# A new order for all engines in the 256-token pair stage, and sums written back into PSUM

## The chip, the cores and the metric

The kernel runs on one core of a Trainium2 chip. Its engines run their own instruction streams, each in order, and wait for one another by semaphores: TensorE (PE in the profile; PEld is its weight load), VectorE (DVE), ScalarE (ACT), GpSimd (POOL) and SyncE (SP, which here only issues DMAs). The metric is the device time of one execution in microseconds (us).

## The reference

A Fourier mixing layer over 8 x 3008 tokens of 256 channels is followed by a gated feed-forward network:

```python
X = np.fft.rfft(x, axis=1)
...                                   # complex linear map, soft threshold, inverse transform
gate = 1.0 / (1.0 + np.exp(-(x @ w_gate)))
val = x @ w_val
return (gate * val @ w_out).astype(np.float32)
```

Here x has 24064 tokens, w_gate and w_val are 256 x 1536 and w_out is 1536 x 256. The Fourier part and the first 4608 tokens of the network fill the first 1025 us or so. The other 19456 tokens go through the pair stage, and the change lies there.

## The kernel before

The pair stage takes 38 pairs of 2 x 256 tokens (NPR). For each pair it runs NH = 6 slots, one for each block of 256 hidden units, so there are 228 slots (NU). In a slot both matrix products of the network are done by a seven-product scheme for 2 x 2 blocks (Strassen's, in Winograd's form) instead of eight products. All values are kept as a high part and a remainder (fp32r), so each product of two blocks takes three matmuls: high by high, high by remainder, remainder by high.

In this text M1 to M7 are the first layer's products of a slot (`first`, each 2 x 3 = 6 matmuls of 128 x 256), and s1 to s7 the second layer's (`second`, 3 matmuls each). That makes 7 x 6 + 7 x 3 = 63 matmuls a slot.

- The first layer accumulates in four PSUM banks of 512 columns: M1 then M2 into bank a (pa), M5 into bank c (pc), M6 and M3 into bank b (pb), M7 and M4 into bank d (pd). ScalarE copies between banks, which the scheme needs as starting values: a to b behind M1 (here called seedb), b to d behind M6 (seedd), both in `seed`.
- Out of the banks come four hidden blocks. Each bank half pair is gate and value: the gate goes through a sigmoid on ScalarE (g11, g21 and so on), the product of gate and value is VectorE's (h11, h21, h12, h22). For the second column M5 must be added first: `take_m5` copies bank c into an SBUF tile m5, and `column2` adds it to bank d and to bank b (here X22 and X12), into the SBUF tile xg. One activation (`gate2`) and one product (`h2`) of 512 columns follow.
- GpSimd makes the four sums of hidden blocks that the second layer needs (`hsum`, S1, S3, S2, S4).
- Then the operands are split: ScalarE casts the high part (`hi`: hiX, hiG, hiS; tiles hpX, hpG, hpS), VectorE subtracts for the remainder (`lo`: loX, loG, loS).
- The second layer accumulates over the six slots of a pair in four more banks (acc). At a pair's end they are evicted (`evict1` to `evict4`): ScalarE copies, VectorE sums, three stores on SP and one adding store on GpSimd's queue.
- During three slots of each pair the next pair's input tile ypair is prepared (`prep_steps`): GpSimd sums, a cast on ScalarE, a remainder on VectorE.

The order of the stage is written out by hand in `slot(k)`, under a manual schedule: slot k issues the first layer of block k, sums, casts and remainders of block k-1, and the second layer of block k-2. On TensorE the order is M1, M5, s1, s2, M6, M2, s4, M7, M3, s7, s6, s5, M4, s3. M4 adds to bank d, which X22 must have read.

Of the kernel before, what the change touches and what calls it, by code (L numbers as in the profile page):

```python
# [26 lines left out]
HW = 256  # L27
# [83 lines left out]
def tile_fft_mix_ffn(ctx: ExitStack, tc, x, w_r, w_i, b_r, b_i, w_one, w_out, mf, mi, mis, fa, fb, mf0, fa0, out):  # L111
# [529 lines left out]
    def prep_steps(p, sub_):  # L641
        g = nc.gpsimd

        def sums(i):
            y = held["y", p]
# [12 lines left out]
        def split(v, names):  # L658
            v = v().rearrange("p a n -> p (a n)")
            t = p4.tile([P, 2, len(names) * HW], F32R, tag=f"xop{len(names)}", bufs=NXB if len(names) == 2 else 2,  # L660
                        name=names[0])
            nc.scalar.copy(t[:, 0], v)
            sub_(t[:, 1], v, t[:, 0])
            xs[p].update(halves_of(t, names))

        return [lambda: sums(1), lambda: split(lambda: held["y", p][:, 1], ("a12", "a22")),
                lambda: sums(3), lambda: split(lambda: held["y", p][:, 0], ("a11", "s3")),
                lambda: (sums(2), sums(4)), lambda: split(lambda: held["s", p], ("s1", "s2", "s4"))]

    hx, hop, accs = {}, {}, {}  # L670
    NU = NPR * NH
# [16 lines left out]
    def second(k, *names):  # L688
        if not 0 <= k < NU:
            return  # L690
        p, fp = divmod(k, NH)
        if p not in accs:
            accs[p] = [psg.tile([P, 512], F32, tag="acc", bufs=2, name="acc") for _ in range(2)]
        w = weights2(fp)
        for name in names:
            b, h = ACC[name]
            if b == len(accs[p]):
                accs[p] += [bank("acc2", "l2", L2_BANKS) for _ in range(2)]
            o = accs[p][b][:, h * HW:(h + 1) * HW]
            xn, wn = PRODUCTS[name]  # L700
            (hh, hl), (wh, wl) = hop[k].pop(xn), w[wn]
            for l, r in ((wh, hh), (wh, hl), (wl, hh)):
                start = fp == 0 and name in (1, 4, 6, 3) and l is wh and r is hh
                nc.tensor.matmul(o, l, r, start=start, stop=l is wl, skip_group_check=True)  # L704
# [8 lines left out]
    def gate(o):  # L713
        nc.scalar.activation(o, o, AF.Sigmoid)  # L714

    def gate11(k):
        g = hx[k, "G"] = p5.tile([P, 2, HW], F32, name="gh", bufs=2)
        nc.scalar.activation(g[:, 0], bank_a[:, :HW], AF.Sigmoid)

    def h11(k):  # L720
        g = hx[k, "G"]
        nc.vector.tensor_mul(g[:, 0], g[:, 0], bank_a[:, HW:])  # L722

    def gate21(k):
# [13 lines left out]

    def gate2(k):
        gate(hx[k, "X"][:, 0])  # L740

    def h2(k):
        x = hx[k, "X"]
        nc.vector.tensor_mul(x[:, 0], x[:, 0], x[:, 1])  # L744

    def hsum(k, i, e):

        x, g = hx[k, "X"], hx[k, "G"]
        if i == 1:
            hx[k, "S"] = p5.tile([P, 3, HW], F32, name="hs", bufs=2)  # L750
            e.tensor_add(hx[k, "S"][:, 0], g[:, 1], x[:, 0, 1])  # L751
# [4 lines left out]
        else:  # L756
            e.tensor_sub(hx[k, "S"][:, 2], x[:, 0, 0], hx[k, "S"][:, 1])  # L757

    def parts_of(k, what):
        v = hx[k, "X"][:, 0] if what == "X" else hx[k, what]  # L760
        return v.rearrange("p a n -> p (a n)")
# [17 lines left out]
    def ev_tile():  # L779
        return p5.tile([P, 7 * HW + PAD], F32, name="ev", bufs=1)[:, :7 * HW].rearrange("p (a n) -> p a n", n=HW)  # L780

    def evict1(p):
        ev = held["ev", p] = ev_tile()
        nc.scalar.copy(ev[:, 0:2].rearrange("p a n -> p (a n)"), accs[p][0])
        nc.sync.dma_start(out_of(p)[:, 0, :HW], ev[:, 0])

    def evict2(p):
        ev, acc = held["ev", p], accs[p]
        nc.vector.tensor_add(ev[:, 5], acc[2][:, :HW], ev[:, 0])
        nc.vector.tensor_add(ev[:, 6], acc[1][:, HW:], ev[:, 5])  # L790
        for ct, lot, i in (0, 1, 6), (1, 0, 5), (1, 1, 6):
            nc.sync.dma_start(out_of(p)[:, ct, lot * HW:(lot + 1) * HW], ev[:, i])
        nc.scalar.copy(ev[:, 2], acc[1][:, :HW])

    def evict3(p):
        ev, acc = held["ev", p], accs[p]
        nc.scalar.copy(ev[:, 4], acc[2][:, HW:])
        nc.vector.tensor_add(ev[:, 3], acc[3][:, :HW], ev[:, 4])

    def evict4(p):  # L800
        nc.gpsimd.dma_start(out_of(p), held["ev", p][:, 1:5].rearrange("p (t a) n -> p t (a n)", t=CT), accum_op=ALU.add)

    def evict_last(p):
        ev, acc = held["ev", p], accs[p]
        add = nc.vector.tensor_add
        add(ev[:, 5], acc[2][:, :HW], ev[:, 0])
        add(ev[:, 6], acc[1][:, HW:], ev[:, 5])
        nc.gpsimd.tensor_add(ev[:, 1], ev[:, 0], ev[:, 1])
        add(ev[:, 2], acc[1][:, :HW], ev[:, 6])
        nc.sync.dma_start(out_of(p)[:, 0], ev[:, 1:3].rearrange("p a n -> p (a n)"))  # L810
        add(ev[:, 5], acc[2][:, HW:], ev[:, 5])
        add(ev[:, 4], acc[2][:, HW:], ev[:, 6])
        add(ev[:, 3], acc[3][:, :HW], ev[:, 5])
        nc.sync.dma_start(out_of(p)[:, 1], ev[:, 3:5].rearrange("p a n -> p (a n)"))

    def slot(k):

        v, g = nc.vector, nc.gpsimd
        live, before = k < NU, 0 < k <= NU
        p, e = divmod(k, NH)  # L820
        q = k - 2
        ends = q >= 0 and q % NH == NH - 1
        begins = q > 0 and q % NH == 0
        qp = q // NH
        last = k >= NU
        steps = None
        if live and p + 1 < NPR:
            if e == 0:
                load_y(p + 1)
                held["prep", p + 1] = prep_steps(p + 1, sub)  # L830
            steps = held["prep", p + 1]
        if live and k:
            first(k, 1)
            seed(bank_b, bank_a)
            first(k, 5)
        if begins:
            evict2(qp - 1)
        if before:
            for i in 1, 3, 2, 4:
# [430 lines left out]
```

## Time and profile before

| | before |
|---|---|
| time, median of 3 runs | 2844.3 us (2842.35 to 2847.09) |
| the profiled execution | 2846.19 us, span 2844.4 us |
| PE busy | 2744.1 us, 96% of the span |
| PEld, DVE, ACT, POOL busy | 88%, 72%, 62%, 41% |
| mean granted TensorE clock | 0.995 |

The span is the time from the first to the last instruction in the profile. The shares are means over the whole program, which has stages of different limits. From about 1070 us on all is pair stage. Matmuls are pipelined, and the profile models their ends: the duration of one is longer than the distance to the next.

### The profile page before, as it was taken

The page shows a single profiled execution, that of the slowest core. Times are in us where ns is not written, and L with a number is a line of the kernel's source. Part 1 is how long each engine was busy: PE and PEld are TensorE (multiplying, and loading weights), DVE is VectorE, ACT ScalarE, POOL GpSimd, SP SyncE. Part 2 cuts the span into 40 slices and gives each one's busy share as a digit, 9 for nine tenths or more (in the row PEclk, how much of TensorE's full clock was granted, in tenths as well). Part 3 has the DMA queues.
Part 4 walks back from the last instruction along what each step waited for, and adds up shares of the span by engine and source line. Part 5 has one row for each costly group of instructions (what it writes and reads, how often), then busy time and mean ns, then how long its engine had stood idle before and what let it go on. Part 6 is the DMA issues. An engine that isn't in the chain of part 4 may idle for free.

```text
span 2844.4 us, 60508 instructions
## 1 busy us (share of the span) xinstructions
PE 2744.1 (96%) x24208; PEld 2508.0 (88%) x24208; DVE 2059.9 (72%) x3240; ACT 1757.1 (62%) x3302; POOL 1153.9 (41%) x1399
## 2 busy tenths in 40 slices
PE   8999999999999999999999999999999999999998
PEld 6678888888998789999999999999999999999998
DVE  5777887777776257777777777777777777777777
ACT  4665655555655356666666666666666666666665
POOL 0231021336000025555555555555555555555554
PEclk9999999999999999999999999999999999999999
DMA  9877656776555731111111111111101111101111
GB/s 288 258 239 197 176 170 172 222 210 209 167 158 164 211 87 27 42 25 44 25 44 25 44 25 44 25 44 25 44 23 46 23 46 23 46 23 45 24 38 25
DMA packets 200873, 268.29 MB, mean 94 GB/s; under 512 B 19664, under 2 KB 152272, under 8 KB 200592
## 3 DMA queue, kind: packets, MB, share of 16 engines
q1 hardware_dynamic: 179504, 220.04, 26.1%
q0 software_dynamic: 20832, 44.31, 7.3%
q8 instruction: 191, 3.13, 0.5%
q14 instruction: 90, 0.74, 0.1%
q10 hardware_dynamic: 256, 0.07, 0.0%
HBM read 137.33 MB, written 127.01 MB: 93 GB/s over the span
## 4 chain that ended last, share of the span: by engine, by line
PE 50%; DVE 25%; POOL 12%; ACT 6%; issue 4%; DMA 3%; SPq 0%; DVEq 0%; ACTq 0%; POOLq 0%
PE pd L684 6%; PE acc L704 6%; PE pa L684 5%; PE pb L684 5%; PE pm L307 5%; DVE xg L736 4%; POOL gh L755 3%; PE pc L684 3%; DVE xg L744 2%; PE pb L274 2%; DVE gh L722 2%; PE pia L390 2%; DVE hpG L772 2%; POOL hs L751 2%; DVE hpS L772 2%
## 5 line engine op out<-in xcount | busy, mean ns | idle before, releaser
L751 POOL TENSOR_TENSOR hs<-gh,xg 128x256 f32<-128x256 f32 x227 | 167.2, 737 | 790.7 <-DVE gh L729 790.7
L772 DVE TENSOR_TENSOR hpG<-gh,hpG 128x512 fp32r<-128x512 f32 x228 | 241.5, 1059 | 258.1 <-ACT hpG L768 258.1
L684 PE MATMUL pd<-a,th 128*128 128x256 f32 x1824 | 366.5, 294 | 50.3 <-DVE xg L736 41.6
L684 PEld LDWEIGHTS pd<-a,th 128*128 128x128 f32 x1824 | 275.6, 188 | 101.4 <-DVE xg L736 88.7
L684 PE MATMUL pa<-a,w1h 128*128 128x256 f32 x1824 | 336.7, 278 | 0.0
L772 DVE TENSOR_TENSOR hpX<-xg,hpX 128x512 fp32r<-128x512 f32 x228 | 197.9, 868 | 157.1 <-ACT hpX L768 157.1
L684 PEld LDWEIGHTS pa<-a,w1h 128*128 128x128 f32 x1824 | 275.9, 188 | 0.0
L755 POOL TENSOR_TENSOR gh<-gh 128x256 f32<-128x256 f32 x227 | 247.0, 1088 | 17.8
L684 PE MATMUL pd<-a,tl 128*128 128x256 f32 x912 | 253.8, 278 | 0.0
L684 PE MATMUL pa<-a,w1l 128*128 128x256 f32 x912 | 252.7, 277 | 0.0
L772 DVE TENSOR_TENSOR hpS<-hs,hpS 128x768 fp32r<-128x768 f32 x228 | 244.6, 1073 | 0.0
L704 PE MATMUL acc<-hpS,w 128*128 128x256 f32 x1368 | 234.3, 280 | 0.0
L757 POOL TENSOR_TENSOR hs<-xg,hs 128x256 f32<-128x256 f32 x227 | 214.2, 944 | 17.8
L768 ACT CAST hpS<-hs 128x768 fp32r<-128x768 f32 x228 | 192.8, 845 | 46.4 <-POOL hs L757 44.8
L714 ACT ACTIVATE xg<-xg 128x512 f32<-128x512 f32 x228 | 144.0, 632 | 116.4 <-DVE xg L736 112.7
L707 ACT COPY pd<-pb 128x512 f32<-128x512 f32 x228 | 130.7, 573 | 135.0 <-ACT hpX L768 91.8
L684 PE MATMUL pb<-s,th 128*128 128x256 f32 x912 | 175.9, 286 | 20.1 <-ACT pb L707 20.1
L704 PEld LDWEIGHTS acc<-hpS,w 128*128 128x128 f32 x1368 | 192.5, 188 | 0.0
L307 PE MATMUL pm<-w_sb,xsh 128*128 128x256 f32 x1008 | 184.6, 285 | 2.2 <-ACT xsh L290 1.6
L707 ACT COPY pb<-pa 128x512 f32<-128x512 f32 x228 | 131.3, 576 | 87.5 <-PE pa L684 87.5
L768 ACT CAST hpG<-gh 128x512 fp32r<-128x512 f32 x228 | 141.7, 621 | 62.6 <-POOL gh L755 62.0
L684 PEld LDWEIGHTS pa<-a,w1l 128*128 128x128 f32 x912 | 171.6, 188 | 0.0
(214 smaller groups left out, 8444.0 us busy)
## 6 DMA issues: line engine op xcount, KB each, us to landing
zf<-zd SPq DMA_DIRECT2D x96, 256.0 KB, 3.7
vf<-vd SPq DMA_DIRECT2D x128, 192.0 KB, 3.8
vd<-vz SPq DMA_DIRECT2D x85, 256.0 KB, 2.8
ypair<-yd SPq DMA_DIRECT2D x38, 512.0 KB, 3.7
yd<-yf SPq DMA_DIRECT2D x103, 188.0 KB, 3.5
out_dram<-ev SPq DMA_DIRECT2D x149, 128.0 KB, 1.8
out_dram<-ev POOLq DMA_DIRECT2D x37, 512.0 KB, 5.8
xf<-in_x_dram SPq DMA_DIRECT2D x80, 192.0 KB, 4.3
```

The lines of the kernel that those rows point to most:

```text
L274: nc.tensor.matmul(pb[:, ct, i], zf[:, i, ct * P:(ct + 1) * P], m[:, i], start=True, stop=True)
L307: nc.tensor.matmul(o, l, r, start=(i == 0), stop=(i == len(mms) - 1))
L684: nc.tensor.matmul(o[:, i * HW:(i + 1) * HW], l, r, start=start, stop=l is wl, skip_group_check=True)
L704: nc.tensor.matmul(o, l, r, start=start, stop=l is wl, skip_group_check=True)
L707: nc.scalar.copy(to, o)
L714: nc.scalar.activation(o, o, AF.Sigmoid)
L736: nc.vector.tensor_add(hx[k, "X"][:, :, i], o.rearrange("p (i n) -> p i n", i=2), hx[k, "m5"].rearrange("p (i n) -> p i n", i=2))
L751: e.tensor_add(hx[k, "S"][:, 0], g[:, 1], x[:, 0, 1])
L755: e.tensor_sub(g[:, 1], g[:, 0], g[:, 1])
L757: e.tensor_sub(hx[k, "S"][:, 2], x[:, 0, 0], hx[k, "S"][:, 1])
L768: nc.scalar.copy(t[:, 0], parts_of(k, what))
L772: sub(t[:, 1], parts_of(k, what), t[:, 0])
```

## The change

The order of a slot is no longer written as code but as a table, ORDER. Each entry is a step and an offset: in slot k the step is done for block k + offset. `slot` walks the table for all engines. Four things are different.

- The order on every engine. loX and s3 move one slot later than before (offsets -2 and -3), h21 moves behind the slot's end (offset -1), loG and loS move behind X12, X22, h12 and h22.
- `column2`, `gate2` and `h2` are gone. `add_m5` adds m5 to bank d and writes the sum into bank c (X22), and adds it to bank b in place (X12); both results stay in PSUM. Gates and products of the second column are then taken from there in halves of 256 columns, as g12, h12, g22 and h22, by the functions `gate` and `times` that all four blocks now share. The SBUF tile xg of 4 x 256 columns becomes xh of 2 x 256.
- Preparation is cut into three steps for three engines (`sums`, `hi_y`, `lo_y`), and GpSimd's sums come one slot ahead of the cast that reads them.
- Evictions are single steps of the table. The accumulators keep fixed banks, and the starting matmul of a bank is found from a set (`begun`). Two unread pad tiles change place.

The core of the diff:

```diff
+ORDER = (
+    ("h21", -1), ("M1", 0), ("seedb", 0), ("s3", -3), ("loX", -2), ("M5", 0), ("hiX", -1), ("s1", -2),
+    ("ev2", -3), ("M6", 0), ("m5", 0), ("M2", 0), ("S1", -1), ("S3", -1), ("seedd", 0), ("s2", -2),
+    ("g11", 0), ("M3", 0), ("M7", 0), ("ev2a", -3), ("S2", -1), ("ev3a", -3), ("s4", -2), ("pACT", 0),
...
-    def column2(k, i):
...
-        nc.vector.tensor_add(hx[k, "X"][:, :, i], o.rearrange("p (i n) -> p i n", i=2),
-                             hx[k, "m5"].rearrange("p (i n) -> p i n", i=2))
-
-    def gate2(k):
-        gate(hx[k, "X"][:, 0])
-
-    def h2(k):
-        x = hx[k, "X"]
-        nc.vector.tensor_mul(x[:, 0], x[:, 0], x[:, 1])
+    def place(at):
+        return {"11": ("G", 0, bank_a), "21": ("G", 1, bank_d), "12": ("X", 0, bank_b), "22": ("X", 1, bank_c)}[at]
+
+    def gate(k, at):
+        what, i, o = place(at)
+        nc.scalar.activation(pair_of(k, what)[:, i], o[:, :HW], AF.Sigmoid)
+
+    def times(k, at):
+        what, i, o = place(at)
+        g = pair_of(k, what)[:, i]
+        nc.vector.tensor_mul(g, g, o[:, HW:])
+
+    def add_m5(k, to, o):
+        nc.vector.tensor_add(to, o, hx[k, "m5"])
...
+    PREP = {1: "X", 3: "G", 5: "S"}
...
+        elif name == "X22":
+            add_m5(k, bank_c, bank_d)
+        elif name == "X12":
+            add_m5(k, bank_b, bank_b)
...
     def slot(k):
...
+        for name, off in ORDER:
+            if 0 <= k + off < NU:
+                step(name, k + off)
```

VectorE in a slot without preparation, before: hpX, hpG and hpS are the remainders loX, loG and loS of the block before; gh<-gh,pa is h11, the two sums into xg are X22 and X12; then h2 and h21.

```order
L772 TENSOR_TENSOR hpX<-xg,hpX 128x512 [waits Activation_49]
L772 TENSOR_TENSOR hpG<-gh,hpG 128x512 [waits Activation_49]
L722 TENSOR_TENSOR gh<-gh,pa_13156 128x256 [waits Activation_49]
L736 TENSOR_TENSOR xg<-pd_13159,m_19433 128x2x256 [waits PE_49,Activation_49]
L736 TENSOR_TENSOR xg<-pb_13158,m_19433 128x2x256 [waits PE_49]
L772 TENSOR_TENSOR hpS<-hs,hpS 128x768 [waits Activation_49]
L744 TENSOR_TENSOR xg<-xg 128x512 [waits Activation_49]
L729 TENSOR_TENSOR gh<-gh,pd_13159 128x256 [waits Activation_49]
```

The same of after, from h21 of the block before: pb<-pb is X12, pc<-pd is X22, and the two rows into xh are h12 and h22.

```order
L743 TENSOR_TENSOR gh<-gh,pd_13159 128x256 [waits Activation_49]
L773 TENSOR_TENSOR hpX<-xh,hpX 128x512
L743 TENSOR_TENSOR gh<-gh,pa_13156 128x256 [waits DVE_49,Activation_49]
L746 TENSOR_TENSOR pb_13158<-pb_13158,m_19597 128x512 [waits PE_49]
L746 TENSOR_TENSOR pc_13157<-pd_13159,m_19597 128x512 [waits PE_49]
L743 TENSOR_TENSOR xh<-xh,pb_13158 128x256 [waits Activation_49]
L743 TENSOR_TENSOR xh<-xh,pc_13157 128x256 [waits Activation_49]
L773 TENSOR_TENSOR hpG<-gh,hpG 128x512 [waits Pool_49]
L773 TENSOR_TENSOR hpS<-hs,hpS 128x768 [waits Activation_49]
```

loG moved from ahead of h11 to the slot's end, with loS behind it, and h2 became two rows.

TensorE ahead of M4 in the same slot, before: hpG,uh is s7, hpS,uh is s6, hpS,w is s5, and the last row is M4's first matmul.

```order
L704 MATMUL acc<-hpG,ul 128x256
L704 MATMUL acc_20335<-hpS,uh 128x256 x2
L704 MATMUL acc_20335<-hpS,ul 128x256
L704 MATMUL acc_20335<-hpS,w_109 128x256 x3
L684 MATMUL pd_13159<-a_20223,th 128x256 [waits DVE_49]
```

After: hpX,uh is s4, then s5, s7, s6 and M4.

```order
L718 MATMUL acc_13378<-hpX,uh 128x256 x2
L718 MATMUL acc_13378<-hpX,ul 128x256
L718 MATMUL acc_13384<-hpS,w_109 128x256 x3
L718 MATMUL acc_13378<-hpG,uh 128x256 x2
L718 MATMUL acc_13378<-hpG,ul 128x256
L718 MATMUL acc_13384<-hpS,uh 128x256 x2
L718 MATMUL acc_13384<-hpS,ul 128x256
L702 MATMUL pd_13159<-xop,th 128x256 [waits DVE_49]
```

s4 moved in between M7 and M4, and s3, which stood behind M4, now comes behind the next M1; M4 still waits for VectorE.

## Rows read from the trace of the kernel before

**Rows 1.** Table of stretches: pair stage; us, busy us per engine (instructions), granted clock, DMA.

```profile
1100.00:2800.00 1700.00, 1632.83 (x13490) 1572.19 (x13489) 1272.35 (x1925) 1107.03 (x2142) 911.62 (x1035) 1.00 0.15 34
```

**Rows 2.** Timeline of TensorE: start us, duration us, engine, line, operation, out<-in, count.

```profile
1073.12 0.40 PE L684 MATMUL pb<-s,th 128*128 128x256 f32 x2
...
1076.30 0.40 PE L704 MATMUL acc<-hpG,uh 128*128 128x256 f32 x2
...
1080.57 0.39 PE L684 MATMUL pb<-s,th 128*128 128x256 f32 x2
...
1083.63 0.39 PE L704 MATMUL acc<-hpG,uh 128*128 128x256 f32 x2
```

**Rows 3.** Timeline of TensorE: first matmul of M5 in slots 2 and 227.

```profile
1040.98 0.40 PE L684 MATMUL pc<-s,w1h 128*128 128x256 f32 x2
...
2825.57 0.39 PE L684 MATMUL pc<-s,w1h 128*128 128x256 f32 x2
```

**Rows 4.** Chain of waits, 2007 to 2023.5: start us, length us, what.

```profile
2008.23 0.85 ACT s L662
...
2009.10 0.96 DVE s L663
2010.07 0.60 DVE xg L744
2010.66 0.34 DVE gh L729
...
2011.07 0.75 POOL hs L751
...
2011.89 1.07 POOL gh L755
...
2012.99 0.63 ACT hpG L768
...
2014.66 0.61 DVE xg L736
...
2015.32 0.97 PE pd L684 x6
...
2022.84 0.74 PE pd L684 x4
```

**Rows 5.** Timeline: a product's end as ScalarE sees it; a remainder beside GpSimd.

```profile
2017.05 0.28 PE L684 MATMUL pa<-a,w1l 128*128 128x256 f32 x1
...
2017.17 0.39 PE L684 MATMUL pc<-s,w1h 128*128 128x256 f32 x2
...
2017.37 0.57 ACT L707 COPY pb<-pa 128x512 f32<-128x512 f32 x1 [0.57 <-PE pa L684]
...
2828.99 1.27 DVE L772 TENSOR_TENSOR hpG<-gh,hpG 128x512 fp32r<-128x512 f32 x1 [1.39 <-ACT hpG L768]
```

**Rows 6.** VectorE's groups, 1100 to 2800: count, busy us, mean ns, idle before.

```profile
L772 DVE TENSOR_TENSOR hpG<-gh,hpG 128x512 fp32r<-128x512 f32 x215 | 227.9, 1060 | 244.2 <-ACT hpG L768 244.2
...
L744 DVE TENSOR_TENSOR xg<-xg 128x512 f32<-128x512 f32 x214 | 146.1, 683 | 0.0
L736 DVE TENSOR_TENSOR xg<-pd,m 128x512 f32<-128x512 f32 x214 | 145.5, 680 | 0.0
...
L722 DVE TENSOR_TENSOR gh<-gh,pa 128x256 f32<-128x256 f32 x215 | 88.1, 410 | 0.0
```

**Rows 7.** ScalarE's groups, same stretch and columns.

```profile
L714 ACT ACTIVATE xg<-xg 128x512 f32<-128x512 f32 x214 | 135.1, 632 | 105.3 <-DVE xg L736 101.7
...
L707 ACT COPY pb<-pa 128x512 f32<-128x512 f32 x214 | 123.3, 576 | 81.0 <-PE pa L684 81.0
...
L718 ACT ACTIVATE gh<-pa 128x256 f32<-128x256 f32 x215 | 82.4, 383 | 0.0
```

**Rows 8.** Timeline of TensorE at the end of the program.

```profile
2832.05 0.51 PE L704 MATMUL acc<-hpS,w 128*128 128x256 f32 x3
...
2836.57 0.51 PE L704 MATMUL acc<-hpG,w 128*128 128x256 f32 x2 [0.97 <-DVE hpG L772]
```

More of the change, by code (lines that the diff above doesn't have):

```diff
@@ L686, in tile_fft_mix_ffn, with acc_bank, second @@
     ACC = {1: (0, 0), 2: (0, 1), 4: (1, 0), 7: (1, 1), 6: (2, 0), 5: (2, 1), 3: (3, 0)}
-    def second(k, *names):
-        if not 0 <= k < NU:
-            return
-        p, fp = divmod(k, NH)
[L692 to L704, printed above, removed]
+    def acc_bank(b):
+        if b not in accs:
+            accs[b] = psg.tile([P, 512], F32, name=f"acc{b}") if b < 2 else bank(f"acc{b}", "l2", L2_BANKS)
+        return accs[b]
+    def second(k, name):
+        p, fp = divmod(k, NH)
+        b, h = ACC[name]
+        o = acc_bank(b)[:, h * HW:(h + 1) * HW]
+        xn, wn = PRODUCTS[name]
+        (hh, hl), (wh, wl) = hop[k].pop(xn), weights2(fp)[wn]
+        for l, r in ((wh, hh), (wh, hl), (wl, hh)):
+            nc.tensor.matmul(o, l, r, start=(p, b) not in begun, stop=l is wl, skip_group_check=True)
+            begun.add((p, b))
     def seed(to, o):
@@ L812, in evict_last @@
[L812 to L813 removed]
+        add(ev[:, 5], accs[2][:, HW:], ev[:, 5])
+        add(ev[:, 4], accs[2][:, HW:], ev[:, 6])
+        add(ev[:, 3], accs[3][:, :HW], ev[:, 5])
         nc.sync.dma_start(out_of(p)[:, 1], ev[:, 3:5].rearrange("p a n -> p (a n)"))
[L816 to L842 removed]
+    FIRST = (1, 5, 6, 2, 7, 3)
@@ new lines, in step @@
+    def step(name, k):
+        p, e = divmod(k, NH)
+        kind, num = name[0], name[1:]
+        if kind == "M":
+            if k or int(num) not in FIRST:
+                first(k, int(num))
+        elif name in ("seedb", "seedd"):
+            if k:
+                seed(*((bank_b, bank_a) if name == "seedb" else (bank_d, bank_b)))
+        elif kind == "s":
+            second(k, int(num))
+        elif name == "m5":
+            take_m5(k)
+        elif kind == "g":
+            gate(k, num)
+        elif name in ("h11", "h21", "h12", "h22"):
+            times(k, num)
+        elif name == "X22":
+            add_m5(k, bank_c, bank_d)
+        elif name == "X12":
+            add_m5(k, bank_b, bank_b)
+        elif kind == "S":
+            hsum(k, int(num), nc.vector if k == NU - 1 else nc.gpsimd)
+        elif name[:2] == "hi":
+            hi(k, num[1])
+        elif name[:2] == "lo":
+            lo(k, num[1])
+        elif kind == "e":
+            if e == NH - 1 and (p < NPR - 1 or name == "ev1"):
+                evict(p, name)
+        elif p + 1 < NPR and e % 2:
+            if name == "pPOOL":
+                sums(p + 1, *{1: (1, 3), 3: (2, 4), 5: ()}[e])
+            elif name == "pACT":
+                hi_y(p + 1, PREP[e])
+            else:
+                lo_y(p + 1, PREP[e])
```

163 lines of the change are left out of this document (60 added, 103 removed), and 3 rows, old and new, of the table ORDER.

## The prediction, made before the changed kernel was run

> **What bounds the kernel now.** I read first the table of stretches [rows 1]. Between 1100 and 2800 us nothing but the pair stage runs. TensorE's granted clock is 1.00 there, the upper of its two levels (2.4 GHz), and no other engine is full: VectorE is busy 1272 of 1700 us, ScalarE 1107, GpSimd 912. The reader should not stop at TensorE's 1633 us. The durations of matmuls overlap, so the gaps between them nearly vanish in that sum. What one matmul really takes is the distance from start to start [rows 2]. From M6 to the first s7 there are always 27 matmuls (M6, M2, s4, M7, M3). The pair that starts at 1080.57 and ends at 1083.63 needs 3.06 us for them, 0.1133 us each; the pair from 1073.12 to 1076.30 needs 3.18 us, 0.1178 each. So TensorE has two paces, both at the same granted clock. A slot has 63 matmuls: 7.14 us at the quick pace, 7.42 at the slow one.
>
> What a slot takes is read from the first matmul of M5 in two slots [rows 3]: slot 2 at 1040.98 and slot 227 at 2825.57, 225 slots in 1784.6 us, 7.93 us each. So 0.5 to 0.8 us of every slot, 115 to 178 us in all, is TensorE waiting. The chain of waits shows for what [rows 4]. In a slot with operand preparation it never touches TensorE until M4: GpSimd's sums of the next pair, their cast on ScalarE (0.85) and remainder on VectorE (0.96), then h2 and h21, then GpSimd's S1 and S3 (0.75 and 1.07), the cast hiG, the remainder loG, h11, the sum X22, and only then M4 (L684, pd). That is one ring, since the next h21 needs M4's gate. M4 starts at 2015.32 and, in the plain slot that follows, at 2022.84: 7.52 us even without preparation. VectorE stands still in that ring, because loG is queued ahead of h11 and X22 and waits for GpSimd.
>
> **The change part by part.** Multiplications and TensorE's work stay: 63 matmuls a slot. I lay out a plain slot of the new order with the trace's durations, time 0 at M1's first matmul, at the quick pace (0.68 us for a product M, 0.34 for a product s): M1 0, s3 0.68, M5 1.02, s1 1.70, M6 2.04, M2 2.72, s2 3.40, M3 3.74, M7 4.42, s4 5.10, s5 5.44, s7 5.78, s6 6.12, M4 6.46, end 7.14. Other engines see a product 0.21 us after its end: M1's last matmul starts at 2017.05, ends its share at 2017.17, and ScalarE begins at 2017.37 [rows 5]. Then each wait on TensorE is checked.
>
> *M6 and M3 (ScalarE's seeds).* The copy seedb (0.58 us [rows 7]) runs from 0.89 to 1.47; M6 wants it at 2.04, 0.5 to spare. The copy seedd starts when M6 is out, 2.93, and ends at 3.50; M3, which overwrites what it reads, comes at 3.74. Only 0.2 is to spare. This is the tightest place.
>
> *M4 (VectorE's X22).* M2 is out at 3.61, gate g11 ends at 3.99 (0.38), h11 at 4.44 (0.41 [rows 6]). The sum X12 starts when M3 is out, 4.63, and ends at 5.31; X22 starts then, just as M7 is out, and ends at 5.99 (0.68 each). M4 wants it at 6.46: 0.4 to spare. In the kernel before, M4's wait ended at this very sum [rows 4].
>
> *loG, loS and the sums on GpSimd.* Now loG and loS stand at the end of VectorE's slot, behind X22. h12 5.95 to 6.36, h22 to 6.84, loG to about 7.45, loS to about 8.3, then h21 to 8.7, which is 1.5 in the next slot. M5 needs h22 only at 8.16, and seedd needs h21 only at 2.93 of the next slot. From 1.6, GpSimd needs 0.75, 1.07 and two more sums between those two values, plus three handovers of 0.07 [rows 4]: done by 5.5. The cast hiG is due at 3.9, when S3 is out (3.5); hiS at 6.3. So the long ring is now spread over two slots, and each link has slack. The remainder loX moves a slot later and ends by 2.5; s2 wants it at 3.5.
>
> *Halves and PSUM.* One gate of 512 columns (0.632) becomes two of 256 (about 0.38 [rows 7]), and one product of 512 (0.683) two of 256 (0.41 [rows 6]): 0.13 us more on ScalarE, 0.14 more on VectorE a slot. VectorE's starts lie closer than durations, 0.60 for 512 and 0.34 for 256 [rows 4], so its slot costs 4 x 0.60 and 0.96 for the five large operations and 4 x 0.34 for the halves, 4.7 us, plus up to 0.38 for each of three remainders that collides with GpSimd (1.06 in the mean instead of 0.68 [rows 6]), plus at most 0.96 of preparation: 6.8 of 7.14. It fits, and is hidden; without that cover the 0.14 would be 32 us over 225 slots. The trace has no VectorE result written to PSUM. The nearest rows are a VectorE sum that reads PSUM, 0.680 against 0.683 all in SBUF [rows 6], and ScalarE's copy from PSUM into PSUM, 0.576, against 0.632 for its activation of that size in SBUF [rows 7]. I take 0.68; the end upwards is the 1.27 us that a collided loG takes [rows 5], downwards 0.58.
>
> *Preparation and eviction.* Preparation is now behind X22 (at most 0.96 us later for h22, which M5 wants 1.3 later), and GpSimd's sums for it a slot ahead of their cast, so the 0.85 + 0.96 leave the path. Evictions stand where ScalarE and VectorE have 0.5 or more free; their DMAs are queued on SP behind the load of the next pair, as before, and the GpSimd store one slot later, behind S4. Buffers, tile names and the gap tile: nothing.
>
> *Ends.* At the start two FFN products stand ahead of M1 in slot 1 instead of behind M5, and two copies ahead of seedb on ScalarE: 0 to 2 us, I take 0.8. At the end 4.5 us lie between M4's end (2832.05) and s1's second matmul (2836.57) [rows 8]; loX, 0.60 each for the last two slots, now stands in that chain, less three matmuls: 1.2 us more.
>
> **Sum.** Span = 2844.4 - 1784.6 + 225 T + 2.0 = 1061.8 + 225 T. All quick gives T = 7.14 and 2668 us, all slow 7.42 and 2731. A pace seems to hold from one wait of TensorE to the next, and quick stretches are the more frequent, so I take a quarter slow: T = 7.21, 2684 us. The profiled execution is 2846.2 with a span of 2844.4, and the median of the runs is 2844.3, so the span stands for the median: **2684 us**, 160 less.
>
> **Rivals.** (1) *The slow pace stays.* With no wait left to end it, TensorE could sit at 0.1178: 2731 us. For it: it did so for 27 matmuls without a break [rows 2]. Against: the next stretch was quick.
> (2) *A new wait takes the old one's place.* If the 0.2 at M3 or hiG's place ahead of g12 is not enough, TensorE again waits every slot. At the old plain slot's 7.52 us [rows 4] only preparation's excess is won: 1061.8 + 225 x 7.52 = 2754 us.
> (3) *Only gaps can go.* TensorE's busy time leaves 67 us idle in 1700 [rows 1]; over 1784.6 us that is 71, so 2774 us. Start-to-start distances speak against it. The Trainium skill ("Perfetto Trace Analysis", Identifying the Most-Contended Engine) says that matmul busy time is a bad measure of the distance to the roofline, because matmuls are pipelined, and tells to use weight-load time instead; by that rule rival 3 is wrong, and the start-to-start rows here agree.
> (4) *Slower.* The sums written to PSUM are dear. X12 and X22 stand one behind the other, ahead of M4, with 0.4 to spare. If each took d longer, a slot would take 7.21 + 2d - 0.4 + 0.1 (a restart costs one matmul's distance). It passes 7.93 at d = 0.5. At 1.27 us each, d = 0.59, it is 8.09: 2882 us. Against: no row of VectorE's with a PSUM operand is above 0.68. The Trainium skill ("Advanced Engine Details and Errata", The Read-Write Bubble) says that VectorE lies closer to SBUF and ScalarE closer to PSUM, and that small tiles pay a fixed latency each; by it this change goes the wrong way twice, towards rival 4. No row here shows the price of the write; of small tiles rows 6 and 7 show it, the 0.13 and 0.14 above.
> (5) *Nothing happens*, because another ring holds the slot at 7.93. The order of the instructions is changed as written, and I find no such ring: 2844 us.
>
> **How the numbers follow.** Forecast 0.74, rival 1 0.12, rival 2 0.07, rival 3 0.03, rival 4 0.03, rival 5 0.01. A difference of 0.2% (6 us) is about what a measurement of this kernel can tell from none. Faster is 0.74 + 0.12 + 0.07 + 0.03 = 0.96, same 0.01, slower 0.03. The range goes from all quick without the 2 us at the ends, 2666, to the slow pace with a little more, 2735; it leaves out rivals 2 to 5 and part of the first two.
>
> **What would show it.** In the changed kernel's profile M5 starts should lie 7.1 to 7.4 us apart in all six kinds of slot, M4 should have next to no idle time behind VectorE, GpSimd's first sum should still wait for h21, and the sums into PSUM should take 0.6 to 0.75 us. A wait of M3 behind seedd, or of M4 behind the second sum, would show the forecast wrong, and so would 0.118 us as the common distance between matmuls.

## The result and the profile after

The changed kernel takes 2676.4 us in the median of four executions (2664.03, 2671.86, 2680.86, 2707.76), the old one beside it 2845.7. The ratio is 0.939, with an interval of 0.935 to 0.943. The execution of 2707.76 us is left out of that ratio as a slow one; the other three have a median of 2671.9 us, and none but the first has a profile. The profiled execution is that of 2664.03 us, with a span of 2662.3.

The first view is the table of stretches, for the new pair stage, with the columns of [rows 1]: length, then busy time and instructions of PE, PEld, DVE, ACT and POOL, then granted clock, DMA share and GB/s.

```profile
1100.00:2640.00 1540.00, 1540.00 (x13582) 1539.36 (x13582) 1165.76 (x2153) 1170.05 (x2370) 854.85 (x1040) 1.00 0.16 38
```

TensorE is busy in all 1540 us. The weight loads too, 1539 of them; they were at 1572 of 1700 in [rows 1]. For the other engines busy time and slot time both changed. In a slot VectorE is busy for 5.41 us instead of 5.94, GpSimd for 3.97 instead of 4.25, and ScalarE, which now has two gates of 256 columns in place of one of 512, for 5.43 instead of 5.16. As a share of the time VectorE has 76% instead of 75%, GpSimd 56% instead of 54%, ScalarE 76% instead of 65%.

The timeline of TensorE shows the first matmul of M5 in slots 2 and 227, as [rows 3] did before:

```profile
1034.88 0.39 PE L702 MATMUL pc<-xop,w1h 128*128 128x256 f32 x2
...
2642.36 0.39 PE L702 MATMUL pc<-xop,w1h 128*128 128x256 f32 x2
```

That is 1607.5 us for 225 slots, 7.144 each, where it was 7.93. All six kinds of slot take 7.14 (the first of a pair 7.17); before they took 7.52 to 8.58. From one matmul's start to the next's are 0.1133 us in all but some twenty of 14175 cases.

One slot with preparation, in the timeline of all engines (start, duration, engine, line, operation, and in brackets the idle time before it with what ended it):

```profile
2028.04 0.41 DVE L743 TENSOR_TENSOR gh<-gh,pd 128x256 f32<-128x256 f32 x1
...
2028.53 1.12 POOL L753 TENSOR_TENSOR hs<-gh,xh 128x256 f32<-128x256 f32 x1 [1.90 <-DVE gh L743]
...
2029.77 0.57 ACT L722 COPY pd<-pb 128x512 f32<-128x512 f32 x1 [0.47 <-PE pb L702]
...
2030.55 0.39 PE L702 MATMUL pb<-xop,w1h 128*128 128x256 f32 x2
...
2031.43 0.70 DVE L746 TENSOR_TENSOR pb<-pb,m 128x512 f32<-128x512 f32 x1 [0.18 <-PE pb L702]
...
2032.11 0.70 DVE L746 TENSOR_TENSOR pc<-pd,m 128x512 f32<-128x512 f32 x1
...
2033.27 0.39 PE L702 MATMUL pd<-xop,th 128*128 128x256 f32 x2
...
2033.98 0.68 DVE L773 TENSOR_TENSOR hpG<-gh,hpG 128x512 fp32r<-128x512 f32 x1
```

From top to bottom: h21 and S1 of the block before, seedd, M3, X12, X22, M4, loG. seedd ends at 2030.34 and M3 starts at 2030.55. X22 ends at 2032.81 and M4 starts at 2033.27. loG, in the old order ahead of all of these, runs beside M4, and nobody waits for it. TensorE has no idle time in brackets. From M3's to M4's start are 24 matmuls in 2.72 us, 0.1133 each, which is the quick pace of [rows 2].

The groups of VectorE and GpSimd from 1100 to 2640 us (count, busy us, mean ns, idle us before), which answer to [rows 6]:

```profile
L746 DVE TENSOR_TENSOR pb<-pb,m 128x512 f32<-128x512 f32 x216 | 151.1, 700 | 40.0 <-PE pb L702 40.0
L746 DVE TENSOR_TENSOR pc<-pd,m 128x512 f32<-128x512 f32 x216 | 151.1, 699 | 0.0
L773 DVE TENSOR_TENSOR hpG<-gh,hpG 128x512 fp32r<-128x512 f32 x215 | 148.2, 690 | 0.0
...
L753 POOL TENSOR_TENSOR hs<-gh,xh 128x256 f32<-128x256 f32 x216 | 241.5, 1118 | 646.3 <-DVE gh L743 646.3
```

The sums into PSUM take 0.700 us; those into SBUF took 0.680 [rows 6]. The remainder hpG fell from 1060 to 690 ns: in the slot above GpSimd computes nothing beside it. Its S1, 737 ns on the page of before, now takes 1118, beside the remainder hpX. That is the only slowed operation that is left, and there were more before. The groups of GpSimd from 1100 to 2800 us in the kernel before have S3 at 1089 ns:

```profile
L755 POOL TENSOR_TENSOR gh<-gh 128x256 f32<-128x256 f32 x214 | 233.1, 1089 | 16.8
```

S4 took 946 there, and VectorE's other two remainders 867 (hpX) and 1079 (hpS). Now S3 takes 738, S4 742, hpX 681 and hpS 949.

The list of waits from 1100 to 2600 us (who waited for whom, us in total, times, longest):

```profile
PEld pb L702 <- ACT pd L722: 0.6, 4, 0.2
```

It is the only line of the list that names TensorE: M3 behind seedd, four times in 210 slots, 0.6 us together. The longest wait of the list, 627.3 us, is GpSimd's for h21, in every slot as before; TensorE does not wait for it.

### The profile page after: what moved, and what is told of

It is laid out like the page before. It is cut to its first block, busy times and chain, and to the rows that moved or that the text cites. A ratio compares the mean times of both kernels' runs of the same rounds, so it can differ in the third digit from the quotient of the medians.

```text
span 2662.3 us, 60662 instructions
## 1 busy us (share of the span) xinstructions
PE 2633.9 (99%) x24208; PEld 2461.0 (92%) x24208; DVE 1940.6 (73%) x3468; ACT 1817.5 (68%) x3530; POOL 1093.4 (41%) x1399
## 5 line engine op out<-in xcount | busy, mean ns | idle before, releaser
L753 POOL TENSOR_TENSOR hs<-gh,xh 128x256 f32<-128x256 f32 x227 | 253.4, 1116 | 734.3 <-DVE gh L743 734.3
L702 PE MATMUL pd<-xop,th 128*128 128x256 f32 x1824 | 333.0, 276 | 0.8 <-DVE pc L746 0.8
L702 PE MATMUL pa<-xop,w1h 128*128 128x256 f32 x1824 | 332.7, 276 | 0.0
L702 PEld LDWEIGHTS pd<-xop,th 128*128 128x128 f32 x1824 | 274.7, 188 | 1.6 <-DVE pc L746 1.4
L702 PEld LDWEIGHTS pa<-xop,w1h 128*128 128x128 f32 x1824 | 274.8, 188 | 0.1
L702 PE MATMUL pd<-xop,tl 128*128 128x256 f32 x912 | 251.7, 276 | 0.0
L702 PE MATMUL pa<-xop,w1l 128*128 128x256 f32 x912 | 251.7, 276 | 0.0
L759 POOL TENSOR_TENSOR hs<-xh,hs 128x256 f32<-128x256 f32 x227 | 168.5, 742 | 17.8
L702 PEld LDWEIGHTS pd<-xop,tl 128*128 128x128 f32 x912 | 171.2, 188 | 0.0
L702 PEld LDWEIGHTS pa<-xop,w1l 128*128 128x128 f32 x912 | 171.2, 188 | 0.0
```

What stands on the lines that cost most here:

```text
L702: nc.tensor.matmul(o[:, i * HW:(i + 1) * HW], l, r, start=start, stop=l is wl, skip_group_check=True)
L753: e.tensor_add(hx[k, "S"][:, 0], g[:, 1], x[:, 1])
L759: e.tensor_sub(hx[k, "S"][:, 2], x[:, 0], hx[k, "S"][:, 1])
```

## The experiments

The slot times below are mean distances of M5's starts, slots 2 to 227, in the profiled execution; those by kind of slot leave out the first pair and the last two. A slot is called plain if it has no preparation.

### The changed kernel once more

> The changed kernel once more, unchanged, for the pace of TensorE in another execution. Theory A (no wait of TensorE is left, and the quick pace is what a stretch without waits holds): M5 starts 7.14 to 7.16 us apart, 0.1133 us the common distance between matmuls, span near 2662 to 2672. Rival P (the pace changes from execution to execution, and the spread of the four times, 2664 to 2708, is the slow pace): a share of the distances at 0.118, one us of span for each 0.44% of slow matmuls (all slow: 225 x 0.28 = 64 us), so that a run of 2690 would show 40%.

Measured: 2670.1 us (2664.88 to 2682.0), ratio 0.940 (0.937 to 0.942). The profiled execution, 2671.09 us, has 7.144 us a slot, and no stretch at the slow pace. Its M5 of slot 0 starts at 1027.13 us, against 1020.05 in the first profile: the seven microseconds between the two executions lie ahead of the pair stage. In the other kernels here, in which nothing ahead of the pair stage is changed, it is at 1021.31 to 1030.26. Theory A holds for this execution; those without a profile stay open. (By rival P's own 64 us for all slow, one us of span answers to 1.6% of slow matmuls, not to 0.44%; its 40% for a run of 2690 us goes by that.)

### The sums back in SBUF, in the new order

```diff
-        nc.vector.tensor_add(to, o, hx[k, "m5"])
+        nc.vector.tensor_add(pair_of(k, "X")[:, :, i], o.rearrange("p (i n) -> p i n", i=2),
+                             hx[k, "m5"].rearrange("p (i n) -> p i n", i=2))
...                                   # g12, h12: nothing; g22, h22: one gate, one product of 512 columns
```

> The new order with the second column as before: sums into the SBUF tile xg, one gate and one product of 512 columns (g12 and h12 fall away, the gate stands at g22, the product at h22). Theory A (the order is the gain; the PSUM part only fits into slack): M5 starts still 7.14 us apart, 2664 to 2690 us. Rival B (the PSUM write-back and the halves are the gain): half of the gain or more goes, 7.5 us or more, 2750 us or above.

Measured: 2666.3 us in the median, ratio 0.938 (0.936 to 0.939); three executions at 2666.1 to 2666.4 and one at 2730.04. So theory A holds: the PSUM part is worth nothing that can be told from none in the new order, and the new order keeps its gain without it.

The execution of 2730 us was the profiled one. In the timeline of TensorE, M3's and M4's starts, with the same 24 matmuls between them as above:

```profile
2005.39 0.40 PE L702 MATMUL pb<-xop,w1h 128*128 128x256 f32 x2
...
2008.22 0.40 PE L702 MATMUL pd<-xop,th 128*128 128x256 f32 x2
```

2.83 us, 0.118 each. The slow pace held from slot 2 to the end, all slots 7.42 us, with a granted clock of 1.00 in that stretch and only two distances above 0.13 us. So this execution too has no wait of TensorE to speak of; it is longer by its pace. The prediction's "all slow", for the changed kernel, was 2731.

### The PSUM part alone, in the old order

```diff
 def column2(k, i):
-    nc.vector.tensor_add(hx[k, "X"][:, :, i], o.rearrange(...), hx[k, "m5"].rearrange(...))
+    nc.vector.tensor_add((bank_b, bank_c)[i], (bank_b, bank_d)[i], hx[k, "m5"])
...                                   # gate2, h2: two halves each, from banks b and c
```

> The old order with the sums written to PSUM and gates and products in halves: the PSUM part alone. Theory A: the ring through h2 and h21 gets 0.14 us longer on VectorE (two products of 0.41 for one of 0.68) and M5 waits for the second half product, so 7.9 to 8.1 us a slot, 2840 to 2880 us. Rival B: half of the gain or more is there, 2755 us or below.

Measured: 2907.8 us, ratio 1.023 (1.021 to 1.025): slower than the old kernel, and above the range of theory A, which had M5's wait but not its size; rival B is out. The slot takes 8.21 us. The sums into PSUM are not dear here either, 0.69 us. The list of waits names the cause, bank c:

```profile
PEld pc L684 <- DVE xh L742: 132.6, 139, 2.5
```

M5 overwrites bank c, and now has to wait until h22 has read the sum there. In the old order h22 stands behind the preparation, so in the slot where the preparation is longest M5 comes over 2 us late (timeline of TensorE, then the table of stretches; the clock is the third number from the right):

```profile
1093.88 0.28 PE L684 MATMUL pa<-a,w1l 128*128 128x256 f32 x1
1096.22 0.50 PE L684 MATMUL pc<-s,w1h 128*128 128x256 f32 x2 [2.07 <-DVE xh L742]
```

```profile
1096.00:1097.00 1.00, 0.78 (x6) 0.78 (x7) 0.50 (x2) 1.00 (x2) 0.42 (x1) 1.00 0.94 170
...
1098.00:1099.00 1.00, 1.00 (x6) 1.00 (x6) 0.00 (x0) 0.00 (x0) 1.00 (x2) 0.50 0.00 0
...
1100.00:1101.00 1.00, 1.00 (x7) 1.00 (x7) 0.52 (x1) 0.87 (x3) 0.92 (x2) 0.50 0.00 0
1101.00:1102.00 1.00, 1.00 (x10) 1.00 (x10) 0.54 (x3) 1.00 (x2) 0.78 (x1) 1.00 0.00 0
```

TensorE is idle for 2.07 us and starts again at 1096.22; within 2 us the granted clock is at 0.50 instead of 1.00, the lower of its two levels, and stays there for some 3 us. Matmuls then lie 0.21 us apart. In this kernel 17 of 36 gaps of 2.0 to 2.6 us (from start to start) were followed by such a stretch of 15 or 16 matmuls, 263 in all. At 0.1 us more for each that is some 26 us; without them the time would be 2882, next to theory A's upper end.

### loG ahead of h11 again, in the new order

```diff
-    ..., ("S4", -1), ("h11", 0), ("X12", 0), ..., ("h22", 0), ("loG", -1), ("M4", 0), ...
+    ..., ("S4", -1), ("loG", -1), ("h11", 0), ("X12", 0), ..., ("h22", 0), ("M4", 0), ...
```

> The new order, but the remainder loG of the slot before stands ahead of h11 on VectorE again, as in the old order. Theory A (the ring h21, S1, S3, hiG, loG, h11, X12, X22, M4, g21, h21 closes within one slot again): M4 waits for X22, 7.5 to 7.9 us a slot, 2750 to 2840 us, and with preparation a slot ahead the six kinds of slot differ by less than the old 1.06 us. Rival C (preparation ahead of h2 and h21 was the whole cost, loG's place is nothing): 7.14 to 7.2, below 2690 us.

Measured: 2893.5 us, ratio 1.017 (1.016 to 1.019), 8.14 us a slot, 7.79 to 8.37 by kind. One entry of 46 takes back the whole gain and more; the time lies above theory A's range of 2750 to 2840. M4 waits for X22 in every slot, as theory A said, but longer than it said. The timeline of the engines from one loG to the next, 8.13 us apart, shows why:

```profile
2004.56 0.69 DVE L773 TENSOR_TENSOR hpG<-gh,hpG 128x512 fp32r<-128x512 f32 x1 [2.10 <-ACT hpG L769]
...
2006.10 0.69 DVE L746 TENSOR_TENSOR pc<-pd,m 128x512 f32<-128x512 f32 x1
...
2006.82 0.38 ACT L738 ACTIVATE xh<-pc 128x256 f32<-128x256 f32 x1 [0.21 <-DVE pc L746]
...
2007.10 0.83 ACT L769 CAST hpS<-hs 128x768 fp32r<-128x768 f32 x1
...
2007.96 0.96 DVE L773 TENSOR_TENSOR hpS<-hs,hpS 128x768 fp32r<-128x768 f32 x1 [0.30 <-ACT hpS L769]
...
2008.84 0.41 DVE L743 TENSOR_TENSOR gh<-gh,pd 128x256 f32<-128x256 f32 x1
...
2009.33 1.12 POOL L753 TENSOR_TENSOR hs<-gh,xh 128x256 f32<-128x256 f32 x1 [3.48 <-DVE gh L743]
...
2010.53 0.74 POOL L757 TENSOR_TENSOR gh<-gh 128x256 f32<-128x256 f32 x1
...
2012.04 0.62 ACT L769 CAST hpG<-gh 128x512 fp32r<-128x512 f32 x1
...
2012.69 0.69 DVE L773 TENSOR_TENSOR hpG<-gh,hpG 128x512 fp32r<-128x512 f32 x1 [2.84 <-ACT hpG L769]
```

loG, X22 (after h11 and X12), g22, hiS, loS, h21, S1, S3, hiG, loG. The ring that I had written down left out g22, hiS and loS: hiS stands behind g22 on ScalarE, and h21 stands behind loS on VectorE.

### The preparation as before, in the new order

```diff
-    ..., ("pACT", 0), ("hiG", -1), ..., ("X22", 0), ("pPOOL", -1), ("g12", 0), ..., ("s6", -2), ("pDVE", 0), ...
+    ..., ("hiG", -1), ..., ("X22", 0), ("pPOOL", 0), ("pACT", 0), ("pDVE", 0), ("g12", 0), ..., ("s6", -2), ...
...
-                sums(p + 1, *{1: (1, 3), 3: (2, 4), 5: ()}[e])
+                sums(p + 1, *{1: (1,), 3: (3,), 5: (2, 4)}[e])
```

> The new order, but the operand preparation as in the old one: GpSimd's sums stand in the slot of the cast that needs them, the cast behind hiG, the remainder ahead of h12 and h22. Theory A (in slots whose cast needs sums, ScalarE's g12, g22 and g21 stand behind GpSimd's S sums, the preparation sums and the cast, and the next slot's seedb behind those): the two of six slots that wait for sums get 1 to 2 us longer, the others stay at 7.14, mean 7.4 to 7.7 us, 2725 to 2795 us. Rival C2 (only loG's place counts, preparation has slack either way): 7.14 to 7.2, below 2690 us.

Measured: 2716.9 us, ratio 0.955 (0.953 to 0.956), 7.37 us a slot, just below the range. Only one kind of slot gets longer by about 1 us, the one with both sums of the S operand (8.12); where the cast waits for one sum, the slack covers it. M5 then waits for h22 (list of waits), which stands behind ScalarE's cast, and the cast, in the timeline at 2040.71 us, behind 2.12 us of waiting for GpSimd's second sum:

```profile
PEld pc L702 <- DVE xh L743: 33.1, 34, 1.0
```

The preparation's place in the new order, with GpSimd's sums a slot ahead, is thus worth some 47 us here (2716.9 against 2670.1).

### loG behind the sums, in the old order

```diff
             hi(k - 1, "G")
-            lo(k - 1, "G")
...
             column2(k, 0)
+            lo(k - 1, "G")
```

> The old order with one thing moved: the remainder loG behind the two sums of the second column instead of ahead of h11. Theory A: the plain slots (three of six) fall from 7.52 to 7.2 to 7.3 us, since M4's sum no longer waits for GpSimd; in the slots with preparation h2 and h21 still wait for GpSimd's sums, the cast and the remainder, so 8.0 to 8.4 stays there: mean 7.6 to 7.85, 2775 to 2830 us. Rival C (loG's place is all of it): 7.2 in all kinds, below 2700 us. Rival D (the order only works as a whole): no gain, 2835 us or above.

Measured: 2800.1 us, ratio 0.984 (0.982 to 0.986), 7.73 us a slot: plain slots 7.20 to 7.27, slots with preparation 8.09 to 8.48. As theory A said, within 0.1 us. What TensorE still waits for, in the list of waits, is above all X22, now 73 times and in slots with preparation (173 times in the same stretch of the old kernel):

```profile
PEld pd L684 <- DVE xg L736: 40.7, 73, 0.8
```

### M3 one small product earlier, in the new order

```diff
-    ("seedd", 0), ("s2", -2), ("g11", 0), ("M3", 0), ...
+    ("seedd", 0), ("M3", 0), ("s2", -2), ("g11", 0), ...
```

> The new order with M3 one small product (0.34 us) earlier, ahead of s2; the prediction gave M3 0.2 us to spare behind the copy seedd. Theory A (each margin is what the laid-out slot says, and a wait costs what is missing plus one restart): M3 waits 0.13 to 0.2 us and restarts for 0.1 in every slot, 7.37 to 7.45 us, 2715 to 2735 us at the quick pace; with the pace drawn anew after each wait, a quarter slow, 10 to 15 us more. Rival (the wait is made good elsewhere in the slot, or the margin was larger): 7.14 to 7.2, below 2690 us.

Measured: 2763.5 us, ratio 0.971 (0.970 to 0.973), 7.57 us a slot. M3 waits in every slot (list of waits):

```profile
PEld pb L702 <- ACT pd L722: 42.0, 198, 0.2
```

Each wait loses 0.18 us and the matmul after it 0.11, 0.28 in all, so 7.43 at the quick pace: theory A's wait. The time is above its range all the same. The rest, 0.14 a slot, is the pace, and it is not a quarter of the stretches that is slow. Timeline of TensorE, M3's fourth matmul and the next M5, 39 matmuls on, in two slots that follow each other:

```profile
2005.53 0.39 PE L702 MATMUL pb<-xop,w1h 128*128 128x256 f32 x2
...
2009.95 0.39 PE L702 MATMUL pc<-xop,w1h 128*128 128x256 f32 x2
...
2012.97 0.40 PE L702 MATMUL pb<-xop,w1h 128*128 128x256 f32 x2
...
2017.56 0.40 PE L702 MATMUL pc<-xop,w1h 128*128 128x256 f32 x2
```

4.42 us and 4.59 us, 0.1133 and 0.1177 each. So it goes on through the whole stage: slots of 7.517 and 7.617 us take turns. Of the 226 stretches between two waits 113 are quick and 113 slow, strictly in turn.

### M4 two small products earlier, in the new order

The first version moved M4's entry in the table:

```diff
-    ("s5", -2), ("s7", -2), ..., ("X22", 0), ..., ("loG", -1), ("M4", 0), ...
+    ("s5", -2), ("M4", 0), ("s7", -2), ..., ("X22", 0), ..., ("loG", -1), ...
```

M4 thereby also came ahead of X22, whose sum then holds M4's products too, so this is no longer the same computation; X22 waited for M4, and the next M5 for h22.

> The new order with M4 two small products (0.68 us) earlier, ahead of s7 and s6; the prediction gave M4 0.4 us to spare behind the sum X22. Theory A: M4 waits 0.2 to 0.3 us and restarts for 0.1 in every slot, 7.44 to 7.55 us, 2735 to 2760 us at the quick pace, 10 to 15 more if a quarter of the stretches between waits is slow, as in the kernels with a wait in each slot so far. Rival (the margin was larger): 7.14 to 7.2, below 2690. On the pace: if it is drawn at each wait, both paces show within one execution; if it is one per execution, all distances are 0.113 or all 0.118.

Measured: 2792.8 us, 7.69 us a slot, above theory A's range. That is a ring through X22, g22 and h22 and says nothing on M4's margin. The second version moves s7 and s6 behind M4 instead:

```diff
-    ("s5", -2), ("s7", -2), ..., ("s6", -2), ..., ("M4", 0), ("hiS", -1), ...
+    ("s5", -2), ..., ("M4", 0), ("s7", -2), ("s6", -2), ("hiS", -1), ...
```

> The new order with the small products s7 and s6 behind M4, so that M4 comes 0.68 us earlier and nothing else moves (its sum X22 stays ahead of it). The changed kernel's rows give M4 0.46 us to spare behind X22. Theory A: M4 waits 0.2 to 0.3 us and restarts for 0.1 in every slot: 7.44 to 7.55 us at the quick pace, up to 0.14 more if half of the stretches between waits is slow (as where M3 stood ahead of s2), 2735 to 2790 us. Rival (the margin is larger, or the wait is made good): 7.14 to 7.2, below 2690 us.

Measured: 2756.5 us, ratio 0.969 (0.967 to 0.970), 7.54 us a slot. M4 waits for X22 (list of waits):

```profile
PEld pd L702 <- DVE pc L746: 61.5, 199, 0.3
```

0.28 us a slot for the wait and 0.11 for the restart, 0.39, which is all that the slot lost: 7.144 + 0.39 = 7.53. Theory A. And here none of the 226 stretches between two waits ran at the slow pace, though TensorE waited in all 225 slots.

### The preparation alone, in the old order

```diff
+            return [lambda: split(lambda: held["y", p][:, 1], ("a12", "a22")), lambda: (sums(1), sums(3)),
+                    lambda: split(lambda: held["y", p][:, 0], ("a11", "s3")), lambda: (sums(2), sums(4)),
+                    lambda: split(lambda: held["s", p], ("s1", "s2", "s4")), lambda: None]
...
             h21(k)
+            if steps and 0 < e < 4:
+                rest()
```

`split` now only casts and returns the remainder as `rest`, which comes behind h21; in each slot the cast stands first and GpSimd's sums, for the next slot's cast, behind it.

> The old order with only the preparation moved: GpSimd's sums of the next pair a slot ahead of the cast that needs them, the remainder behind h21 instead of ahead of h2. Theory A (two rings: the preparation's in three of six slots, loG's in all): the slots with preparation fall from 8.2 to 8.6 to 7.5 to 7.8, since the cast (0.85) still stands ahead of gate2, the plain ones stay at 7.52; mean 7.5 to 7.7, 2750 to 2795 us. Rival (loG's ring gives no gain without the other moved first, or the remainder now delays h11): 2820 us or above.

Measured: 2795.9 us, ratio 0.983 (0.982 to 0.985), 7.72 us a slot: plain slots 7.52 to 7.53, slots with preparation 7.77 to 8.08. The upper ends of theory A were 7.7 and 2795 us, and 7.8 for the slots with preparation: the gain is there, a little smaller than the smallest that it allowed.

### Both, in the old order

The edits of the last run and of "loG behind the sums" together.

> The old order with both moved, loG behind the second column's sums and the preparation as in the run before; all else (seeds, the sums on GpSimd, loX, the second column in SBUF in full width) as in the old kernel. Theory A (these two are the gain): plain slots 7.2, slots with preparation 7.2 to 7.6, mean 7.2 to 7.4, 2685 to 2730 us. Rival E (the rest of the new table carries a third or more of the gain): 7.45 or more, 2740 us or above.

Measured: 2795.7 us, ratio 0.983 (0.982 to 0.985), 7.72 us a slot. Theory A falls and rival E holds: the rest of the new table carries more than a third of the gain. Each of the two gave 46 or 48 us, both together give no more than one. Plain slots are at 7.20 to 7.23, but slots with preparation at 7.74 to 8.65. The chain of waits (start, length, what) through a plain slot shows a ring that I had not seen:

```profile
2000.72 0.34 DVE gh L737
...
2001.14 0.75 POOL hs L759
...
2001.95 1.08 POOL gh L763
2003.05 0.62 ACT hpG L776
2003.67 0.28 ACT gh L726
2003.95 0.48 ACT m L719
2004.46 1.29 DVE xg L744 x2
2005.75 0.60 DVE hpG L780
2006.35 0.87 DVE hpS L780
2007.22 0.60 DVE xg L752
2007.82 0.34 DVE gh L737
```

From h21 to the next h21, 7.1 us, and TensorE is not in it. On ScalarE the cast hiG, which waits for GpSimd's S3, stands ahead of gate11 and the copy m5. So both sums of the second column wait for GpSimd through ScalarE, though loG is out of their way. And h21 stands behind loS and h2. A plain slot hides this ring just so; anything more in it, as the preparation, makes the slot longer.

### ScalarE's hiG behind m5 as well

```diff
-            hi(k - 1, "G")
...
             take_m5(k)
+            hi(k - 1, "G")
```

> The old order with loG and the preparation moved as in the run before, and one thing more: ScalarE's cast hiG, which waits for GpSimd's third sum, behind gate11 and the copy m5 instead of ahead of them. In the run before, the plain slot of 7.20 us was the ring h21 0.34, S1 0.75, S3 1.08, hiG 0.62, gate11 0.28, m5 0.48, the two sums 1.29, loG 0.60, loS 0.87, h2 0.60 and back to h21. Theory A2 (that ring was the last one; without gate11, m5 and the two sums it is 5.2 us): plain slots 7.14 at the quick pace, slots with preparation 7.14 to 7.4, mean 7.14 to 7.3, 2670 to 2715 us. Rival E2 (the cast of the preparation and the remainder of hiS ahead of h2 still hold the slots with preparation): plain slots 7.14 to 7.2, the others 7.6 to 8.2, mean 7.4 to 7.7, 2725 to 2795 us.

Measured: 2736.4 us, ratio 0.963 (0.961 to 0.964), 7.46 us a slot: plain slots 7.20 without a wait, those with preparation 7.42 and 7.63, and 8.17 where the eviction falls into the same slot. One line gives 59 us more. Theory A2 holds for the plain slots alone. X22 is gone from TensorE's waits; what is left is M7 behind seedd and, with 10.8 us in 33 slots, products into bank b behind seedb:

```profile
PEld pd L692 <- ACT pd L715: 22.1, 40, 0.6
```

It lies in the range of rival E2. By the chain of waits into a slot of 8.16 us VectorE's queue is the path, with the two sums, loG, loS, h2, h21, the remainder of the preparation and the eviction's sums one behind the other, and then ScalarE's, with the cast hiX ahead of seedd.

The plain slots take 7.20 us, not 7.14, though TensorE waits for nothing in them. The timeline of TensorE in one of them has M5, the first matmul of s6, 42 matmuls on, and the next M5, another 21 on:

```profile
2005.76 0.39 PE L692 MATMUL pc<-s,w1h 128*128 128x256 f32 x2
...
2010.52 0.39 PE L712 MATMUL acc<-hpS,uh 128*128 128x256 f32 x2
...
2012.96 0.39 PE L692 MATMUL pc<-s,w1h 128*128 128x256 f32 x2
```

The 42 lie 0.1133 us apart, the 21 behind them 0.1162. The longer distances are the same eleven or so in each such slot, from s6 over s5, M4 and s3 to M1, here and in the two other kernels with loG moved in the old order. The new order on TensorE, with s5 and s7 ahead of s6 and with s3 behind the next M1, does not show them. At 0.06 us in each of 225 slots that is some 13 us of the gain which no wait accounts for. Why these matmuls lie further apart is open.

Which of the remaining moves (loX and s3 a slot later, halves of h2, the evictions' places) brings the rest of the last 66 us to the changed kernel wasn't tried, and none of these kernels is measurably faster than it.

## Why the prediction was right, point by point

The forecast was 2684 us, the range 2666 to 2735, and faster.

**The bound.** Right. The old slot was a ring with GpSimd in it, TensorE was not the bound, and with the ring spread over two slots TensorE is. In the old trace the 225 slots lost 156 us to distances between matmuls above 0.135 us, the waits and restarts, and 22 us to distances between those and 0.1133; in the new one both are below 1 us. Of the ring the prediction named one place, loG ahead of h11 and X22 on VectorE. That place is worth 46 us alone, and putting it back into the new order costs over 220. It left out a second one, hiG ahead of gate11 and m5 on ScalarE, worth 59 us where the others were already moved. The changed table has m5 ahead of seedd and hiG behind g11, and my laid-out slot took that over without pointing it out: that the forecast came out in spite of it is the table's merit and not that of my account. An edit of just the two places that my account named, loG and the preparation, gives 2796 us.

**The slot time.** Forecast 7.21, measured 7.144. With 7.144 the prediction's own sum gives 2669 us, against 2664.03 and 2671.09 for the two profiled executions. The term that was mis-sized is the pace. The prediction shows no count for its quarter; in the old trace 56 of 299 stretches of 20 or more matmuls between waits are slow. Nor does a pace hold from one wait to the next as a rule: in the old order it also changes without a wait, around M4 (in the kernel with hiG moved, 29 of 105 changes). But the new order has next to no waits, and there the pace didn't change: the profiled executions were quick throughout (7.144, twice, in the changed kernel) or slow throughout (7.42, once, with the sums in SBUF). So a mean pace was the wrong form for the term, and that the median lies within 12 us of 2684 is in part luck. Rival 1 looks less like another case beside the forecast than like its other face: it named 2731, and 2730.04 was measured once, though not on the changed kernel itself. Three executions of the changed kernel without a profile, 2680.86, 2682.0 and 2707.76 us, lie in between; what they were made of isn't known.

**The margins.** M3 behind seedd 0.2 forecast, 0.21 measured; M4 behind X22 0.4 forecast, 0.46 measured. Both were then overdrawn, by products of 0.34 and 0.68 us moved ahead: the slot grew by 0.28 at the quick pace and by 0.39, each time what was missing plus a handover of some 0.05 and a restart of 0.11. Rival 2 needed that and did not come.

**PSUM and halves.** The sums cost 0.700, I took 0.68. Hidden, as said: with the sums in SBUF the time is the same, and the 0.26 us a slot by which ScalarE's busy time grew are hidden too. Rival 4's price d was 0.02, far from 0.5. The Trainium skill ("Advanced Engine Details and Errata", The Read-Write Bubble) puts VectorE closer to SBUF than to PSUM; the rows here show a difference of that sign, 0.020 us in 0.68, for a sum of 512 columns. The cost that the PSUM part can have lies elsewhere: it ties M5 to h22. The laid-out slot gave 1.3 us to spare there, and in the new order that was enough. In the old order h22 stands behind the preparation, M5 waits, and the kernel gets slower.

**Preparation.** It left the path, as said; 47 us of the gain when it is put back, 48 when it is moved alone. But the two gains don't add, because each edit leaves the other's ring, or the third, as the bound.

**Busy time as a bound.** Rival 3 (2774) is out. The Trainium skill ("Perfetto Trace Analysis", Identifying the Most-Contended Engine) says to judge TensorE's headroom by the busy share of its weight loads, beside the share of its peak rate, and not by matmul time. The weight loads were idle 128 of 1700 us before [rows 1], 134 over the 1784.6 us of 225 slots; the stage got 177 shorter. Nearer than matmul time with 71, and still short. A slow pace doesn't show as idle weight loads: in the execution with all slots at 7.42 us they were busy for 1664.8 of 1666 us.

**The ends.** Forecast 2.0 us more, measured 1.35: from slot 0 to slot 2 14.83 us instead of 14.56 (I took 0.8 more), behind slot 227's M5 19.89 instead of 18.81 (I took 1.2). What I had not counted on is that the stages ahead, which the change doesn't touch, scatter by up to 10 us from one execution to another; the profiled one had M5 of slot 0 6.4 us earlier. The sum is then 2844.4 - 6.4 + 0.3 - 177.1 + 1.1 = 2662.3.

## What to carry to other kernels

When a ring through several engines bounds a stage, write down every instruction that stands ahead of a link on its own queue, on all engines: the ring moves to the next queue as soon as one is cleared, so two single moves gave some 47 us each, both together no more, and the whole order 170. A forecast made as a slot with start times and margins can be tested margin by margin, and an overdrawn margin cost what was missing plus a handover and one restart. Where TensorE shows two paces and nothing in the new order would end a stretch, forecast two times with a chance each rather than a mean.

## What the runs showed of the hardware

- **A pace that holds.** At a granted clock of 1.00 the same 256-column matmuls lie 0.1133 or 0.118 us apart. In the new order without waits the pace of the first slots held through all 228 in three profiled executions (1600 us, 64 us of difference). With a wait in every slot it took turns (M3 earlier), or stayed quick throughout (M4 earlier, second version), or was slow in 56 of 225 stretches (loG ahead of h11), and each change lay at a wait. In the old order it also changed without one, around M4, where the distances of some eleven matmuls a slot were 0.116 to 0.123 us in the mean. What decides it is open.
- **The clock after a wait.** In the old order with the sums in PSUM, 17 of 36 gaps of 2.0 to 2.6 us between matmuls were followed by 15 or 16 matmuls at half the clock, all of them behind gaps of 2.32 us or more; other gaps as long were not. No such stretch followed the 36 gaps of 1.15 to 1.48 us in the old order with loG and the preparation moved.
- **VectorE beside GpSimd.** Operations of the two that run beside each other take longer, and which one pays differs. In the mean of the old order hpG took 1060 ns, hpS 1079, hpX 867, GpSimd's S3 1089 and S4 946. In the new order S1 alone is slowed, from 737 to 1118 ns beside hpX, which itself takes 681; the others are at 690, 949, 738 and 742. The loss became smaller, and what is left lies on an engine that TensorE does not wait for.
